# The attention output's copy one step later, and the score tails in the transposes' PSUM banks

## The chip, the cores and the metric

The kernel runs on one core of a Trainium2 chip. TensorE (PE) does the matmuls and writes them into PSUM, VectorE (DVE) finds the 32 largest scores of each row, ScalarE (ACT) copies out of PSUM and does exponentials, GpSimd (POOL) works from SBUF to SBUF, and SyncE (SP) issues nearly all DMAs. Each engine runs its own instructions strictly in the order in which they were written; engines meet only through semaphores. The metric is the device time of one execution in microseconds, as a median of several runs.

## The reference: what is computed

The first block is attention with a top-k mask, for 8 batches and 8 heads of 576 tokens of 64 channels:

```python
scores = scale * np.matmul(q, k.transpose(0, 1, 3, 2))
kth = np.partition(scores, -32, axis=-1)[..., -32:-31]
scores = np.where(scores >= kth, scores, -1e9)
attn = softmax(scores)                       # with 1e-9 added to the sum
attn_out = np.matmul(attn, v)
```

Its output, as x of 8 batches by 576 tokens by 512 channels, goes through a Fourier mix and a feed-forward block:

```python
u = x + np.real(np.fft.fft(np.fft.fft(x, axis=1), axis=2))
un = (u - mean(u)) / np.sqrt(var(u) + 1e-6)
out = u + np.maximum(un @ w_ch1, 0.0) @ w_ch2     # 512 -> 2048 -> 512
```

All of it is float32.

## The kernel before

**Tiles and steps.** Two heads of one batch form a pair: 32 pairs, 4 to a batch. A pair's query rows are cut into 9 items (IN_PAIR, line 326): four tiles of 128 rows for each of the two heads, and one item, with no head of its own (`e is None`, called the None item here), that holds the 64 leftover rows of both heads. The main loop (from line 1485) runs one step per item, 288 in all. Step i is called step r of its pair here, with r = i mod 9.

DVE needs 4 MAX8 and 3 MATCH_REPLACE8 over 576 scores for each item: it finds eight maxima at a time and strikes them out. In step i it does the second half of item i and the first half of item i+1 (line 1582). The scores are therefore made three steps ahead: step i issues `scores(i + 3)`.

**Scores.** For each item, a matmul makes the scores of the first 512 keys in one of two PSUM banks of the pool ps_s (tag "sp", line 398, or line 383 for the None item in four quarter-sized matmuls), and ACT copies them into the SBUF tile S (lines 401 and 390). The scores of the last 64 keys of both heads, the tails, come from one matmul of their own, `sp_t` (line 368), which takes a bank of the same two, and two small ACT copies (line 372). Both heads of a tile are made in one step, and their tails in the next; the None item's scores and tails are made in the same step, which is step 1 of a pair. So in step 1 the order of banks is: scores of the first half (bank A), scores of the second half (bank B), tails (bank A again). PE can write the tails only when ACT has copied both quarters of bank A.

The steps with a tails matmul are 7, 0, 1, 3 and 5 of a pair.

**Other users of PSUM.** Pool ps_t, two banks (tag "tp"), is for transposes: q and k of the next pair are transposed there by `prep` (line 294), q in step 0 and k in step 5 of a pair. Each takes four transposes into one bank and a fifth, for the leftover rows, into the other, each followed by ACT copies (line 316 for q, 318 and 322 for k). Pool ps_o, one bank (tag "o"), holds the attention's output and then its transposes. Three more banks serve the feed-forward block.

**From the mask to the attention's output.** In the first batch, in pair 7 and in the last pair, the masked and exponentiated tile P is transposed on PE through ps_t. In pairs 4 to 6 and 8 to 30 (`by_dma`, line 435) it is transposed by DMA instead. There, for an item:

- POOL scales the bounds after DVE's last maximum, at the end of step i (`bounds`, line 427, tile nt);
- in step i+1 ACT makes the mask first of all (line 443, waits for nt), POOL subtracts (line 446), and ACT takes the exponential at the end of its step (line 454);
- in step i+2, after the next item's mask, ACT splits the result into two planes of 16 bits (line 467), and SP sends them to DRAM;
- in step i+3 SP issues the transposing DMA into the tile PT (`turn`, line 501);
- at the end of step i+4, `attend` (line 559, 20 matmuls) multiplies PT with v into the bank "o". That is done for two chunks of a pair: chunk 0 (320 rows) at the end of step 8, chunk 1 (256 rows) at the end of step 3 of the next pair.

Right after `attend`, in the same step, `attended` (line 568) issues on ACT the copy of that bank into the SBUF tile xT, for chunk 0 two small copies of the denominators, and the sum with 1e-9 into rd. It also puts DVE's reciprocal of rd on a list that is run at the end of the next step. In the next step `to_tokens` (line 589) turns xT back with 3 or 2 transposes into the bank "o" (tile tpx), placed behind the scores and the transposes of q or k, and DVE multiplies them with rd into x at the end of that step (lines 603 and 610; in batch 1 ACT does it a step later). `to_tokens` is held back while x still belongs to an earlier batch that has not been written out; the chunks wait in a list (`pending`) and are taken one per step, in steps that have no `attend`.

**What ACT is given in one step**, in order: mask of the last item, the two planes of the item before it, the copies of this step's scores or tails, one-step-late work on a list `out_next` (used in the first batch alone), the copies of q or k, the copies of Fourier and feed-forward work, the exponential, and where there is an `attend` its copy last:

```python
if n == n_mask:                       # after the scores of the step
    run(i, "act")
    for fn in out_next:
        fn()
```

**The feed-forward work.** The matmuls of the Fourier mix and of the feed-forward block of a finished batch (lines 961, 988, 1027, 1158) are cut into units of about 2 us, and a planner spreads them over the steps of the next batch so that PE's work per step comes out even. It counts the costs of `attend` and `to_tokens` in the step of the `attend`. After the last item only this work is left.

Of the kernel before, what the change touches and what calls it, by code (L numbers as in the profile page):

```python
# [9 lines left out]
F32 = mybir.dt.float32  # L10
# [63 lines left out]
def kernel(  # L74
# [21 lines left out]
    NPB = H // 2  # L96
    NPAIR = B * NPB
# [23 lines left out]
    ps_s = ctx.enter_context(tc.tile_pool(name="ps_s", bufs=2, space=bass.MemoryType.PSUM))  # L121
    ps_t = ctx.enter_context(tc.tile_pool(name="ps_t", bufs=2, space=bass.MemoryType.PSUM))
# [7 lines left out]
    def bank(shape, name, hold=False):  # L130
        n = banks_free.pop(0)
        t = ps_m.tile(shape, F32, name=name, tag=f"m{n}", bufs=1)
        if not hold:
            banks_free.append(n)
            return t
        return t, lambda: banks_free.append(n)
# [19 lines left out]
    late_now, late_next = [], []  # L156
# [170 lines left out]
    PER_PAIR = len(IN_PAIR)  # L327
# [6 lines left out]
    def scores(i, part):  # L334

        if not 0 <= i < N:
            return 0.0
        pair, t, e = items[i]  # L340
        qT, kT = qT_of[pair], kT_of[pair]
        rows = ROWS[t]
        if part == 0:
            for n in range(1 if e is None else 2):
                Ssb[i + n] = attp.tile([P, S], F32, name=f"S_{i + n}", tag="S", bufs=6)
        q_cols = slice(P * t, P * t + rows)


        plain = (slice(0, NF * P), slice(NF * P, S))
        tails_first = (slice(TAIL, S), slice(0, TAIL))  # L350
        if e is None:
            to = [
                (Ssb[i], slice(TAIL * h, TAIL * (h + 1)), *(tails_first if h and by_dma(i) else plain))
                for h in range(2)
            ]
        else:
            to = [
                (Ssb[i], slice(0, P), *plain),
                (Ssb[i + 1], slice(0, P), *tails_first),
            ]  # L360
        if part == 1:

            copy = nc.scalar.copy if i else nc.vector.tensor_copy
            shape, name = [P, NF * P], f"sp_{i}_t"
            sp = ps_s.tile(shape, F32, name=name, tag="sp") if i else bank(shape, name)

            q_end = P * t + rows
            nc.tensor.matmul(  # L368
                sp[:, 0:P], lhsT=qT[:, q_end - P:q_end], rhs=kt_t, start=True, stop=True
            )  # L370
            for h, (s_t, r, _, tails) in enumerate(to):
                copy(out=s_t[r, tails], in_=sp[P - rows:P, TAIL * h:TAIL * (h + 1)])  # L372
            return 0.3
        if e is None and i >= PER_BATCH:

            half = NF * P // 2
            sps = [
                ps_s.tile([P, NF * P], F32, name=f"sp_{i}_{h}", tag="sp") for h in range(2)
            ]
            for g in range(2):  # L380
                for h in range(2):
                    hd = slice(D * h, D * (h + 1))
                    nc.tensor.matmul(
                        sps[h][TAIL * g:TAIL * (g + 1), 0:half],
                        lhsT=qT[hd, q_cols], rhs=kT[hd, half * g:half * (g + 1)],
                        start=True, stop=True,
                    )
            for h, (s_t, r, keys, _) in enumerate(to):
                for g in range(2):
                    nc.scalar.copy(  # L390
                        out=s_t[r, keys][:, half * g:half * (g + 1)],
                        in_=sps[h][TAIL * g:TAIL * (g + 1), 0:half],
                    )
            return 0.6
        for h, (s_t, r, keys, _) in enumerate(to):
            hd = slice(D * h, D * (h + 1))
            sp = ps_s.tile([P, NF * P], F32, name=f"sp_{i}_{h}", tag="sp")
            nc.tensor.matmul(  # L398
                sp[r], lhsT=qT[hd, q_cols], rhs=kT[hd, :], start=True, stop=True
            )  # L400
            nc.scalar.copy(out=s_t[r, keys], in_=sp[r])  # L401
        return 1.04
# [24 lines left out]
    def bounds(i):  # L427

        if i < N:
# [2 lines left out]
                out=Nt[i], in0=M8.pop(i)[:, 0:TOPK:TOPK - 1], in1=cc, op=ALU.mult  # L432
            )

    def by_dma(i):

        pair = i // PER_PAIR
        return NPB <= pair < NPAIR - 1 and pair != 2 * NPB - 1

    def mask(i, then=None):  # L440

        w = Wk[i]
        nc.scalar.activation(out=w, in_=Ssb[i], func=AF.Relu, scale=-FAR, bias=Nt[i][:, 1:2])  # L443
        if then is not None:
            then()
        nc.gpsimd.tensor_tensor(out=w, in0=Ssb[i], in1=w, op=ALU.subtract)  # L446
        if not by_dma(i):
            Ssb.pop(i)

    def expo(i):  # L450
        pair, t, e = items[i]
        w = Wk[i]
        c = DEN_COL[(t, e)]
        nc.scalar.activation(  # L454
            out=Ssb[i] if by_dma(i) else w, in_=w, func=AF.Exp, bias=Nt.pop(i)[:, 0:1],
            accum_out=den_t[pair % 3][:, c:c + 1],
        )
# [92 lines left out]
    def attend(pair, ch, c0=0, c1=None):  # L550

        c1 = CW[ch] if c1 is None else c1
        pt, vv = PT[pair, ch], v_of[pair]
        if c0 == 0:
            o_of[pair, ch] = ps_o.tile([P, CW[0]], F32, name=f"o_{pair}_{ch}", tag="o")
        o = o_of[pair, ch]
        for c in range(NC):
            for e in range(2):
                nc.tensor.matmul(  # L559
                    o[D * e:D * (e + 1), c0:c1],  # L560
                    lhsT=vv[:, c, e, :],
                    rhs=pt[:, NF if c == NF else (NF + 1) * e + c, c0:c1],
                    start=(c == 0),
                    stop=(c == NC - 1),
                )
        return (c1 - c0) / 115.0

    def attended(pair, ch, late):

        o, w = o_of.pop((pair, ch)), CW[ch]  # L570
        PT.pop((pair, ch))
        xT = attp.tile([P, CW[0]], F32, name=f"xT_{pair}_{ch}", tag="xT", bufs=4)
        nc.scalar.copy(out=xT[:, 0:w], in_=o[:, 0:w])
        xT_of[pair, ch] = xT
        den = den_t[pair % 3]
        if ch == 0:
            for h in range(2):
                nc.scalar.copy(
                    out=den[TH * h:TH * (h + 1), 5:6],
                    in_=den[TAIL + TH * h:TAIL + TH * (h + 1), 4:5],  # L580
                )
        c0, n = (0, 6) if ch == 0 else (6, 4)
        rd = small.tile([P, 6], F32, name=f"rd_{pair}_{ch}", tag="rd", bufs=6)

        nc.scalar.activation(out=rd[:, 0:n], in_=den[:, c0:c0 + n], func=AF.Copy, bias=1e-9)
        late.append(lambda: nc.vector.reciprocal(out=rd[:, 0:n], in_=rd[:, 0:n]))
        rd_of[pair, ch] = rd
# [699 lines left out]
    for c in range(2):  # L1287
        scores(0, c)
    prep("q", 0, ((2, NF), (NF, NC)))
    scores(2, 0)  # L1290


# [142 lines left out]
    queue, waiting, pending, written, now, out_next = [], [], [], set(), [0], []  # L1435
    step_us = 6.0

    def chunk_at(i):

        for tile in (i - 4, i - 3, i - 2):  # L1440
            r = tile % PER_PAIR
            if PER_BATCH <= tile < N and r in (4, 8):
                if i - tile == (4 if by_dma(tile) else 2 if tile == 2 * PER_BATCH - 1 else 3):
                    return tile // PER_PAIR, r // 8
        return None, None
# [38 lines left out]
    i, carry = 0, 0.0  # L1484
    while i < N + 5 or plan or queue or sums:
# [18 lines left out]
        if i < N and i % PER_PAIR == 5:  # L1504
            preps.append(lambda: prep("k", pair_of + 1))
        fixed.append(lambda: scores(j - 1, 1) if e == 1 else scores(j, 0))
        n_mask = 0
        fixed += preps
# [19 lines left out]
        if short:  # L1528
            fixed += tok
            pair, r = divmod(i - 1, PER_PAIR)  # L1530
# [39 lines left out]
        pair, ch = chunk_at(i)  # L1570
        if pair is not None:
            cost += attend(pair, ch)
            attended(pair, ch, late_next)
            pending.append((i + 1, pair, ch))
        if i < N:
            if q_step:
                load_nat("k", pair_of + 1)
# [67 lines left out]
```

## Time and profile before

| | |
|---|---|
| median of 3 runs | 1886.04 us (1885.32 to 1888.74) |
| the profiled execution | 1888.63 us |
| its span, first to last instruction | 1886.8 us |
| busy share of PE, DVE, ACT, POOL | 91%, 84%, 69%, 48% |
| DVE's work on one item, from 4 MAX8 and 3 MATCH_REPLACE8 | about 5.2 us |
| 400 to 1000 us: PE, DVE busy | 559.19 and 552.95 of 600 us |
| 1000 to 1700 us: PE, DVE busy | 681.09 and 634.93 of 700 us |
| mean granted TensorE clock | 0.954 |

The profile gives for every instruction its engine, its line in the kernel, the tile that it writes and those that it reads, its start and its duration. Where an engine stood idle before an instruction, the idle time stands in brackets behind it together with the one who ended it: "[1.64 <-ACT S L390]" means idle for 1.64 us until the ACT instruction of line 390, which writes S, was done. The view of waits sums these over a stretch: total us, number, longest. "PEld" are the weight loads of PE, which run beside its matmuls. A wait for several semaphores is put down to the one that came last. The profiled execution lies 2.6 us above the median.

### The profile page before, as it was taken

The page shows a single profiled execution, that of the slowest core. Times are in us where ns is not written, and L with a number is a line of the kernel's source. Part 1 is how long each engine was busy: PE and PEld are TensorE (multiplying, and loading weights), DVE is VectorE, ACT ScalarE, POOL GpSimd, SP SyncE. Part 2 cuts the span into 40 slices and gives each one's busy share as a digit, 9 for nine tenths or more (in the row PEclk, how much of TensorE's full clock was granted, in tenths as well). Part 3 has the DMA queues.
Part 4 walks back from the last instruction along what each step waited for, and adds up shares of the span by engine and source line. Part 5 has one row for each costly group of instructions (what it writes and reads, how often), then busy time and mean ns, then how long its engine had stood idle before and what let it go on. Part 6 is the DMA issues. An engine that isn't in the chain of part 4 may idle for free.

```text
span 1886.8 us, 26907 instructions
## 1 busy us (share of the span) xinstructions
PE 1724.3 (91%) x8134; PEld 1089.6 (58%) x8134; DVE 1582.2 (84%) x3301; ACT 1295.8 (69%) x3104; POOL 912.1 (48%) x1278
## 2 busy tenths in 40 slices
PE   6667699889899999999999999999999999999999
PEld 3344365355456654566456665566556655667677
DVE  7999999799899999997998898999999899862110
ACT  6878658577787777776777677777787678652100
POOL 4768644454745366354643465355544464341012
PEclk8778899899899999999999999999999999999999
DMA  5333026661557755575465845586467655440132
GB/s 166 103 97 108 20 63 160 166 156 32 137 149 193 186 130 137 140 202 140 122 157 136 225 121 128 142 220 156 120 160 179 179 132 144 120 117 6 51 110 72
DMA packets 516576, 249.16 MB, mean 132 GB/s; under 512 B 398288, under 2 KB 506448, under 8 KB 516432
## 3 DMA queue, kind: packets, MB, share of 16 engines
q1 hardware_dynamic: 515664, 247.23, 50.6%
q8 instruction: 65, 1.06, 0.2%
q14 instruction: 79, 0.65, 0.1%
q10 hardware_dynamic: 768, 0.21, 0.0%
HBM read 93.63 MB, written 84.74 MB: 95 GB/s over the span
## 4 chain that ended last, share of the span: by engine, by line
PE 63%; DVE 12%; ACT 10%; POOL 6%; DMA 4%; issue 3%; SPq 2%; POOLq 0%; DVEq 0%; ACTq 0%
PE hp L961 23%; PE cp L988 8%; PE o L559 7%; DVE m L422 5%; PE sp L398 5%; DVE wk L424 5%; PE cw L1158 3%; PE yp L750 3%; PE cv L1158 3%; PE cp L1027 2%; POOL wk L446 2%; ACT wk L443 2%; ACT wk L467 2%; PE sp_t L368 2%; PE mp L811 1%
## 5 line engine op out<-in xcount | busy, mean ns | idle before, releaser
L446 POOL TENSOR_TENSOR wk<-S,wk 128x576 f32<-128x576 f32 x288 | 408.6, 1419 | 572.2 <-ACT wk L443 570.0
L422 DVE MAX8 m<-wk 128x8 f32<-128x576 f32 x864 | 626.4, 749 | 6.0
L961 PE MATMUL hp<-unT,w 128*128 128x256 f32 (+1 forms) x2048 | 535.5, 412 | 3.6 <-ACT hT L965 2.8
L961 PEld LDWEIGHTS hp<-unT,w 128*128 128x128 f32 x2048 | 378.5, 191 | 134.5 <-issue 30.1
L424 DVE MATCH_REPLACE8 wk<-m,wk 128x576 f32<-128x576 f32 x576 | 427.4, 742 | 0.0
L467 ACT COPY wk<-S 128x576 uint16<-128x576 uint16 x468 | 288.7, 666 | 0.1
L443 ACT ACTIVATE wk<-S,nt 128x576 f32<-128x576 f32 x288 | 222.2, 772 | 73.0 <-POOL nt L431 72.1
L988 PE MATMUL cp<-w,hT 128*128 128x512 f32 x512 | 244.6, 614 | 0.0
L422 DVE MAX8 m<-S 128x8 f32<-128x576 f32 x288 | 213.9, 743 | 31.9 <-ACT S L372 31.8
L559 PE MATMUL o<-PT,v 128*64 128x256 f32 (+3 forms) x1440 | 205.1, 429 | 19.3 <-DMA PT<-planes 15.4
L424 DVE MATCH_REPLACE8 wk<-m,S 128x576 f32<-128x576 f32 x288 | 213.5, 741 | 0.0
L965 ACT ACTIVATE hT<-hp 128x320 f32<-128x320 f32 (+1 forms) x256 | 103.6, 409 | 155.3 <-PE hp L961 154.5
L454 ACT ACTIVATE S<-wk,nt 128x576 f32<-128x576 f32 x234 | 182.6, 781 | 39.9 <-POOL wk L446 38.9
L398 PE MATMUL sp<-kT,qT 64*128 64x512 f32 (+1 forms) x528 | 183.1, 693 | 12.2 <-ACT means L1346 5.1
L559 PEld LDWEIGHTS o<-PT,v 128*64 128x64 f32 x1440 | 118.0, 158 | 105.0 <-issue 35.5
L988 PEld LDWEIGHTS cp<-w,hT 128*128 128x128 f32 x512 | 93.4, 195 | 109.5 <-issue 107.7
L401 ACT COPY S<-sp 128x512 f32<-128x512 f32 (+1 forms) x264 | 141.6, 586 | 18.5 <-PE sp L398 17.6
L1103 POOL TENSOR_TENSOR hT<-hT 128x512 f32<-128x512 f32 x64 | 81.3, 1274 | 99.0 <-ACT hT L965 86.2
L368 PEld LDWEIGHTS sp_t<-kt,qT 128*128 128x128 f32 x320 | 55.7, 198 | 100.6 <-ACT S L390 44.2
L368 PE MATMUL sp_t<-kt,qT 128*128 128x128 f32 x320 | 72.1, 308 | 45.0 <-ACT S L390 29.8
L431 POOL TENSOR_TENSOR nt<-m,cc 128x2 f32<-128x2 f32 x288 | 58.9, 205 | 111.9 <-DVE m L422 108.9
L1158 PE MATMUL cw<-w,hT 128*128 128x256 f32 x448 | 105.7, 383 | 0.7 <-issue 0.6
(160 smaller groups left out, 2137.9 us busy)
## 6 DMA issues: line engine op xcount, KB each, us to landing
planes<-wk SPq DMA_DIRECT2D x208, 288.0 KB, 2.7
w<-w_parts SPq DMA_DIRECT2D x82, 512.0 KB, 4.7
space<-in_moe_w_ch_dram SPq DMA_DIRECT2D x32, 512.0 KB, 3.7
nat<-in_q_dram SPq DMA_DIRECT2D x128, 64.0 KB, 2.4
v<-in_v_dram SPq DMA_DIRECT2D x64, 128.0 KB, 3.0
out_dram<-x SPq DMA_DIRECT2D x32, 256.0 KB, 2.6
nat<-in_k_dram SPq DMA_DIRECT2D x62, 128.0 KB, 2.9
planes<-wk SPq DMA_DIRECT2D x52, 144.0 KB, 2.6
```

The lines of the kernel that those rows point to most:

```text
L368: nc.tensor.matmul(sp[:, 0:P], lhsT=qT[:, q_end - P:q_end], rhs=kt_t, start=True, stop=True)
L398: nc.tensor.matmul(sp[r], lhsT=qT[hd, q_cols], rhs=kT[hd, :], start=True, stop=True)
L422: ops.append(lambda src=src, m8=m8: nc.vector.max(out=m8, in_=src))
L424: ops.append(lambda src=src, m8=m8: nc.vector.match_replace(w, m8, src, NEG))
L443: nc.scalar.activation(out=w, in_=Ssb[i], func=AF.Relu, scale=-FAR, bias=Nt[i][:, 1:2])
L446: nc.gpsimd.tensor_tensor(out=w, in0=Ssb[i], in1=w, op=ALU.subtract)
L454: nc.scalar.activation(out=Ssb[i] if by_dma(i) else w, in_=w, func=AF.Exp, bias=Nt.pop(i)[:, 0:1], accum_out=den_t[pair % 3][:, c:c + 1],)
L467: nc.scalar.copy(out=words[:, half, :], in_=src[:, half, :])
L559: nc.tensor.matmul(o[D * e:D * (e + 1), c0:c1], lhsT=vv[:, c, e, :], rhs=pt[:, NF if c == NF else (NF + 1) * e + c, c0:c1], start=(c == 0) ...
L961: nc.tensor.matmul(hp[:, 0:w], lhsT=w1[:, dt, P * it:P * (it + 1)], rhs=unT[:, dt, 0:w], start=(dt == 0), stop=(dt == NDT - 1),)
L988: nc.tensor.matmul(cp, lhsT=hT[:, it, P * n:P * (n + 1)], rhs=w2[:, it, :], start=(it == 0), stop=(it == NIT - 1),)
L1158: nc.tensor.matmul(dst, lhsT=h()[a][:, kc, :], rhs=rhs_of(kc), start=start and kc == 0, stop=kc == NK - 1, skip_group_check=True,)
```

## The change

Two things change, both only in the pairs whose P is transposed by DMA.

The tails matmul takes a bank of ps_t (tag "tp"), which it then shares with the transposes of q and k, instead of one of ps_s. There are 26 such pairs with 5 tails each, 130 in all.

`attended` is no longer issued in the step of its `attend` but in the next one, after that step's scores, by way of `out_next`; `to_tokens` may come two steps after the `attend` instead of one. The last chunk of a batch keeps the old order. That moves 47 of the 52 chunks of these pairs: chunk 0's copy from the end of step 8 to step 0 and its transposes from step 0 to step 1, chunk 1's copy from the end of step 3 to step 4 and its transposes from step 4 to step 5.

```diff
-            sp = ps_s.tile(shape, F32, name=name, tag="sp") if i else bank(shape, name)
+            if by_dma(i):
+                sp = ps_t.tile(shape, F32, name=name, tag="tp")
+            else:
+                sp = ps_s.tile(shape, F32, name=name, tag="sp") if i else bank(shape, name)
...
+    def pair_by_dma(pair):
+
+        return NPB <= pair < NPAIR - 1 and pair != 2 * NPB - 1
+
     def by_dma(i):
-
-        pair = i // PER_PAIR
-        return NPB <= pair < NPAIR - 1 and pair != 2 * NPB - 1
+        return pair_by_dma(i // PER_PAIR)
...
         pair, ch = chunk_at(i)
         if pair is not None:
             cost += attend(pair, ch)
-            attended(pair, ch, late_next)
-            pending.append((i + 1, pair, ch))
+            if pair_by_dma(pair) and (pair % NPB, ch) != (NPB - 1, 1):
+                out_next.append(lambda pair=pair, ch=ch: attended(pair, ch, late_next))
+                pending.append((i + 2, pair, ch))
+            else:
+                attended(pair, ch, late_next)
+                pending.append((i + 1, pair, ch))
```

## The prediction

> **What bounds the kernel now.** I read the busy time by stretches first, then who waited for whom between 400 and 1680 us, then two timelines.
>
> Stretches (busy us and instructions of PE, PEld, DVE, ACT, POOL, then clock, DMA share, GB/s):
>
> ```profile
> 400.00:1000.00 600.00, 559.19 (x2639) 342.81 (x2638) 552.95 (x1148) 456.83 (x1103) 303.65 (x455) 0.96 0.57 143
> 1000.00:1700.00 700.00, 681.09 (x3296) 434.36 (x3295) 634.93 (x1319) 517.73 (x1236) 347.48 (x504) 0.99 0.60 152
> 1700.00:1800.00 100.00, 99.66 (x444) 67.32 (x442) 19.33 (x53) 20.71 (x52) 9.60 (x34) 1.00 0.08 27
> ```
>
> After 1700 us PE alone is busy, with a fixed remainder. So the end is PE's busy time, which the change leaves alone, plus PE's idle time: 600 - 559.19 = 40.8 us and 700 - 681.09 = 18.9 us in the two stretches where the change acts. Every us of PE idleness added or removed there shows at the end; DVE counts only where its lateness reaches PE through ACT.
>
> Waits from 400 to 1680 us (total, times, longest):
>
> ```profile
> ACT xT L573 <- PE o L559: 80.4, 34, 11.8
> ...
> ACT wk L443 <- POOL nt L431: 64.2, 47, 3.8
> DVE x L603 <- PE tpx L599: 43.2, 16, 6.6
> ...
> PE sp_t L368 <- ACT S L390: 28.1, 19, 3.6
> ...
> DVE rd L586 <- ACT rd L585: 11.2, 6, 6.7
> ...
> PE o L559 <- DMA PT<-planes: 7.5, 4, 2.7
> ```
>
> PE's largest wait is that of the tails for their bank (5.1 us more of it names L401). ACT's largest is for the attention's output: it stands at the copy that ends a step, with the next mask, planes and tails behind it. DVE's largest is for the transposes of xT. PE's wait for late PT is small itself, but sets off some of the others.
>
> **Part 1, the tails' bank.** Step 0 of pair 25, and from 1333 step 1:
>
> ```profile
> 1323.15 0.49 PE L368 MATMUL sp_t<-kt,qT 128*128 128x128 f32 x2
> ...
> 1323.48 0.71 PE L308 MATMUL tpq<-ident,nat 128*128 128x128 f32 x5
> ...
> 1326.29 0.31 ACT L372 COPY S<-sp_t 128x64 f32<-128x64 f32 x2
> ...
> 1333.40 1.52 ACT L390 COPY S<-sp 64x256 f32<-64x256 f32 x4
> ...
> 1334.21 0.49 PE L368 MATMUL sp_t<-kt,qT 128*128 128x128 f32 x2 [1.64 <-ACT S L390]
> 1334.54 1.88 PE L988 MATMUL cp<-w,hT 128*128 128x512 f32 x4
> ```
>
> Removed: I went through the 130 tails of the affected pairs in the timeline. PE's idle time before them sums to 34.3 us: 27.5 before the None items' (step 1), 6.8 before the rest. Not all of it goes. After the change the next scores, in step 2, take the two banks that the None item's copies (L390) free. At 969.02 the tails waited 2.31 us and the scores follow with no unit between, so they would inherit 1.55. Setting for each pair the start of those scores, less the wait saved, against the ends of the L390 copies, 7.9 of the 27.5 us only move and 19.6 go. Removed: 19.6 + 6.8 = 26.4 us.
>
> Added: in ps_t the tails sit next to the transposes of q (step 0) and k (step 5). Bank order there is tails, four transposes in the other bank, and the fifth in the tails' bank: a new wait on L372. At 1323 there is no unit between; the fifth transpose started at 1323.91, and L372 ended at 1326.60. Laying all 26 places of each kind side by side (end of L372 plus 0.06 us of signalling, as in the rows of L390, minus the start of the fifth transpose, where positive) gives 44.3 us for q and 11.9 for k, if ACT keeps its times. These are the upper ends; the lower is nothing, where ACT comes sooner; a gain from a later PE transpose has no row and is excluded. For q ACT does come sooner: xT's copy (0.42), two denominators (0.39) and rd (0.21) leave its way, 1.02 us, and where it idled at xT it can do mask and planes meanwhile. Subtracting 1.02 and that idleness (2.0 at most, mask plus planes) place by place leaves 17.3 us, which I take because its shift is measured. For k nothing gets shorter: ACT there waits for nt (1354.84, 3.14 us), so I take 11.9. Sum of part 1: 17.3 + 11.9 - 26.4 = +2.8 us.
>
> The Trainium skill, "Perfetto Trace Analysis", section "Matmuls", wants independent groups to rotate through different PSUM banks so that copies overlap matmuls. Here either ring has two banks, and the rows show that the new one has a tight place too; by the rule alone the change would save all 34.3 us.
>
> **Part 2, the copy and the transposes a step later.** Per chunk it moves an ACT copy (0.36 to 0.43 us), two of 0.2 (chunk 0 only), one of 0.21, a DVE reciprocal of 0.18, 3 or 2 PE transposes and 2 or 1 DVE products (on ACT in pairs 4 to 6); none is added, and no DMA. On ACT they pass the mask, two planes and the step's score copies. The planes' DMA on SP therefore issues up to 1 us sooner, more where ACT stood, as does POOL's subtraction; SP's order stays. q's copies come no later, being behind both. No wait is added on ACT: "o" is complete before the step's scores.
>
> The bank "o" is held longer. Its next user is normally the same chunk's tpx, a step later; where older chunks are queued it is an older one's tpx in the very step of the copy. At 1016.30 that has room: L372 there began at 1014.02 behind xT, so xT's copy would end near 1013.8. I cost it at nothing; without that cover it would wait about 1 us in some five places. The skill's "PSUM — Partial Sum Buffer", section "Summary: rules for kernel authors", says to evacuate promptly, which speaks against this; no row here shows a bank wait of "o" above 1 us, and by the rule I would add those 5 us.
>
> Late PT makes PE late, and then DVE waits at the transposes. Pair 16, step 0:
>
> ```profile
> 857.96 0.49 PE L368 MATMUL sp_t<-kt,qT 128*128 128x128 f32 x2
> ...
> 858.07 0.42 ACT L573 COPY xT<-o 128x320 f32<-128x320 f32 x1 [11.77 <-PE o L559]
> ...
> 859.18 0.19 DVE L586 RECIPROCAL rd<-rd 128x6 f32<-128x6 f32 x1 [6.71 <-ACT rd L585]
> ...
> 862.81 0.55 PE L599 MATMUL tpx<-ident,xT 128*128 128x128 f32 x3
> ...
> 863.40 0.42 DVE L603 TENSOR_TENSOR x<-tpx,rd 128x256 f32<-128x256 f32 x1 [4.03 <-PE tpx L599]
> ```
>
> Chunk 0's transposes move behind the scores (0.66) and about one unit (1.9 to 2.3) of step 1: 2.9 us later on PE, while DVE has 5.3 us more work before it asks. So each such stall shrinks by up to 2.4 us. Seven are of this kind (551, 601, 799, 858, 1065, 1274, 1477): 1.9 + 2.4 + 5 x 2.4 = 16.3 us. The other stalls at tpx are of chunks held back by `pending`, and stay. Chunk 1 moves behind k's transposes (0.7) and a larger share of units (0.7), 1.4 us later within its step; in five places that had less room (0.42, 1.01, 0.67, 0.66, none) this makes 4.2 us of new stalls. DVE gains 12.1 us.
>
> What reaches PE: in each later batch the next PE wait on ACT (918, 1127, 1334, 1537: some 1.65 each; 656: 1.35) comes from a mask that waits for nt, that is for DVE. With DVE up to 2.4 us earlier, these and the new waits in step 0 shrink by about 1.7 us in five batches: -8.5 us. Its ends: 0, if PE's waits are already counted in part 1, and -12.1.
>
> **Sum.** +2.8 - 8.5 = -5.7 us on the profiled execution's 1888.6 us. That stands 2.6 us above the median of 1886.0, so I put the same difference on the median: 1880.0 us.
>
> **Rivals.**
> 1. Waits only change place: the tails' waits go to the fifth transposes, and DVE's 8.5 us are the same waits counted twice. For it: 17.3 + 11.9 is close to 26.4. Against it: the 2.4 us of DVE are additional. Result +2.8 at the most, 1886 to 1889.
> 2. Slower: PE waits at the fifth transpose for L372. Place: steps 0 and 5, 52 of them. Price: up to 44.3 + 11.9 = 56.2, less 26.4, plus 4.2 of chunk 1, that is +34 us, 1920; at two thirds of that price, 37.5 + 4.2 - 26.4 = +15, 1901. It decides once those places exceed 26.4 + 8.5 = 34.9 us, 0.67 each; I took 0.56. For it: DVE-bound stretches (1323, 1356), where ACT cannot come sooner. Against: the stretches after 858, 1065, 1274, 1477, where ACT idled 5 to 12 us.
> 3. Larger gain: ACT, free during attend, has the tails copied before the fifth transpose everywhere. -26.4 - 12.1 = -38 us, 1848 as the far end, 1860 to 1870 more likely. For it: 80.4 us of ACT idleness at xT. Against: the waits for nt.
>
> **Chances and range.** Forecast 0.42, its own range 1874 to 1884 (the 8.5 us between 5 and 12.1, part 1 within 3); rival 1 0.18; rival 2 0.30; rival 3 0.10. 0.2% is 3.8 us, about what a measurement of this kernel can tell from no change. Faster: 0.37 of the forecast and rival 3, 0.47. Same: 0.05 of the forecast and rival 1, 0.23. Slower: 0.30. Both signs hold weight, so the range takes rival 3 down to 1866 and rival 2 up to 1898, leaving out a tenth on each side.
>
> **What the profile after would show.** Part 1: the wait sp_t on L390 near nothing; new waits of tpq and tpk on L372, some 17 and 12 us; scores L398 on L390 up to 8. Part 2: ACT xT on PE o near nothing, since o is done when ACT arrives; the DVE wait for rd gone; tpx stalls 43 to about 31. PE idle from 400 to 1700 about 54 instead of 59.7 us. Wrong if the fifth transposes wait over 35 us, or if stalls at tpx grow, or if PE's units settle otherwise because the planner sees the transposes' cost a step later.

## The result

The change makes the kernel slower: 1905.05 us (median of 4 runs, 1901.56 to 1911.9) against 1886.87 us (4 runs, 1885.32 to 1888.74), a ratio of 1.0098 with a 95% interval of 1.008 to 1.0115. The forecast was 1880.0 us within 1866 to 1898. The forecast named a gain, and the time lies outside its range; the second rival had named a loss, with 1901 us.

The execution profiled after took 1911.9 us, 6.9 above its median, with a span of 1910.1. The spans of the two profiled executions thus differ by 23.3 us, some 5 more than the medians do; the shifts below are read with that in mind. Line numbers grow by 3 to 5: sp_t is now L371 and its copies L375, the scores L401 and their copies L404 and L393, the mask L448, `attend` L564, tpx L604.

The stretches of the kernel after (busy us and instructions of PE, PEld, DVE, ACT, POOL, then clock, DMA share, GB/s):

```profile
400.00:1000.00 600.00, 540.19 (x2556) 336.28 (x2555) 540.17 (x1120) 441.81 (x1069) 297.14 (x448) 0.94 0.56 140
1000.00:1700.00 700.00, 674.58 (x3268) 431.62 (x3268) 637.21 (x1326) 522.17 (x1243) 346.80 (x503) 0.99 0.60 155
```

PE is idle for 59.8 us of the first and 25.4 of the second, 85.2 in all; it was 59.7 before and the forecast was about 54. DVE loses as well, mostly in the first stretch: 552.95 busy before, 540.17 now.

Waits from 400 to 1680 us in the kernel after:

```profile
ACT wk L448 <- POOL nt L434: 80.9, 59, 4.8
...
DVE m L425 <- ACT S L375: 60.8, 24, 6.7
...
DVE x L608 <- PE tpx L604: 36.2, 20, 6.3
...
ACT S L404 <- PE sp L401: 26.9, 15, 6.1
...
ACT S L375 <- PE sp_t L371: 21.9, 9, 8.7
...
PE tpk L308 <- ACT S L375: 21.6, 9, 6.7
...
PE tpq L308 <- ACT S L375: 20.3, 11, 8.3
...
PE sp L401 <- ACT S L393: 10.3, 8, 2.1
```

PE's wait of the tails for L390 has shrunk from 28.1 to 1.3 us, ACT's for "o" at xT from 80.4 to 6.3 and DVE's for rd from 11.2 to 2.2. New are PE's waits at the fifth transposes of q and k, and DVE's wait for the tails in S has more than doubled (from 270 to 1700 us 31.8 before, 72.5 now). ACT's idleness did not vanish with the copy of xT: part of it now stands at the copies of the tails and of the scores, which PE writes behind the same `attend`.

One place shows why a stop here is worse than the one removed. Step 0 of pair 9, after:

```profile
496.70 0.49 PE L371 MATMUL sp_t<-kt,qT 128*128 128x128 f32 x2
497.03 0.60 PE L308 MATMUL tpq<-ident,nat 128*128 128x128 f32 x4
...
503.77 0.78 ACT L448 ACTIVATE wk<-S,nt 128x576 f32<-128x576 f32 x1 [3.72 <-POOL nt L434]
...
505.59 0.31 ACT L375 COPY S<-sp_t 128x64 f32<-128x64 f32 x2
...
505.89 0.76 DVE L425 MAX8 m<-S 128x8 f32<-128x576 f32 x1 [1.47 <-ACT S L375]
505.95 0.48 PE L308 MATMUL tpq<-ident,nat 128*128 128x128 f32 x1 [8.32 <-ACT S L375]
```

The same step before:

```profile
498.34 0.71 PE L308 MATMUL tpq<-ident,nat 128*128 128x128 f32 x5
...
498.98 0.77 PE L750 MATMUL yp<-fs,fg 128*64 128x145 f32 x8
...
502.72 0.32 ACT L372 COPY S<-sp_t 128x64 f32<-128x64 f32 x2
...
503.02 0.76 DVE L422 MAX8 m<-S 128x8 f32<-128x576 f32 x1 [1.46 <-ACT S L372]
```

ACT can't copy the tails until its mask, which waits for nt, that is for DVE's last maximum of the step before. Before the change that copy stopped only DVE, while PE went through its Fourier units. Now PE's fifth transpose waits for the same copy, with all those units behind it. One late ACT instruction holds PE and DVE at once.

This can be counted. From the bounds of item 36 to those of item 279, in idle stretches of 0.3 us and more, PE and DVE stood idle together for 2.9 us before and 15.1 us after (worked out from the instructions of the two traces).

To see what each place costs PE in all, the trace was summed by tile over the same items (called the stage below): for each matmul the time from the end of PE's work before it to its own end, so that the wait and a slow matmul both count. "cp" is the result of the second feed-forward matmuls. In us:

| | stage | tails sp_t | tpq and tpk | scores sp | cp | all else |
|---|---|---|---|---|---|---|
| before | 1417.6 | 83.3 | 29.8 | 165.5 | 258.5 | 880.5 |
| after | 1438.2 | 39.8 | 83.7 | 156.7 | 265.8 | 892.2 |
| difference | +20.6 | -43.5 | +53.9 | -8.8 | +7.3 | +11.7 |

The tails gave back 43.5 us, of which 35.2 were waits and 8.3 the tails' own matmuls. But the fifth transposes took 53.9. These two places make +10.4 of the +20.6. At cp it is +7.3; there PE's time at a granted clock of 0.50 rose from 18.1 to 35.6 us. Of the +11.7 elsewhere, 6.7 are more idle time before `attend`. What causes these last two was not tested one by one.

### The profile page after: what moved, and what is told of

It reads as the page before. It is cut to its first block, busy times and chain, and to the rows that moved or that the text cites. A ratio compares the mean times of both kernels' runs of the same rounds, so it can differ in the third digit from the quotient of the medians.

```text
span 1910.1 us, 26930 instructions
## 1 busy us (share of the span) xinstructions
PE 1715.6 (90%) x8134; PEld 1093.0 (57%) x8134; DVE 1586.1 (83%) x3301; ACT 1295.7 (68%) x3104; POOL 912.2 (48%) x1278
## 3 DMA queue, kind: packets, MB, share of 16 engines
q8 instruction: 65, 1.06, 0.2%
## 4 chain that ended last, share of the span: by engine, by line
PE 52%; ACT 14%; DVE 11%; POOL 11%; issue 7%; DMA 3%; SPq 1%; POOLq 0%; DVEq 0%; ACTq 0%
PE hp L966 20%; PE o L564 5%; DVE wk L427 5%; PE cp L993 5%; DVE m L425 5%; POOL wk L451 4%; PE sp L401 4%; ACT wk L448 3%; ACT wk L472 3%; PE yp L755 3%; PE cw L1163 3%; PE cv L1163 3%; PE cp L1032 3%; POOL fg L651 2%; ACT S L459 2%
## 5 line engine op out<-in xcount | busy, mean ns | idle before, releaser
L448 ACT ACTIVATE wk<-S,nt 128x576 f32<-128x576 f32 x288 | 222.5, 773 | 93.9 <-POOL nt L434 91.8
L425 DVE MAX8 m<-S 128x8 f32<-128x576 f32 x288 | 214.0, 743 | 72.5 <-ACT S L375 72.5
L993 PE MATMUL cp<-w,hT 128*128 128x512 f32 x512 | 253.4, 633 | 0.0
L564 PE MATMUL o<-PT,v 128*64 128x256 f32 (+3 forms) x1440 | 201.3, 423 | 26.3 <-DMA PT<-planes 10.9
L401 PE MATMUL sp<-kT,qT 64*128 64x512 f32 (+1 forms) x528 | 169.7, 676 | 16.4 <-ACT S L393 10.3
L564 PEld LDWEIGHTS o<-PT,v 128*64 128x64 f32 x1440 | 117.9, 156 | 106.8 <-issue 40.7
L404 ACT COPY S<-sp 128x512 f32<-128x512 f32 (+1 forms) x264 | 141.4, 585 | 38.7 <-PE sp L401 38.0
L1163 PEld LDWEIGHTS cw<-w,hT 128*128 128x128 f32 x448 | 82.4, 190 | 20.9 <-issue 9.3
L527 PE MATMUL tpP<-ident,wk 128*128 128x128 f32 x216 | 41.3, 323 | 58.4 <-ACT wk L459 34.7
```

Of the source, the lines that this page charges most:

```text
L401: nc.tensor.matmul(sp[r], lhsT=qT[hd, q_cols], rhs=kT[hd, :], start=True, stop=True)
L425: ops.append(lambda src=src, m8=m8: nc.vector.max(out=m8, in_=src))
L564: nc.tensor.matmul(o[D * e:D * (e + 1), c0:c1], lhsT=vv[:, c, e, :], rhs=pt[:, NF if c == NF else (NF + 1) * e + c, c0:c1], start=(c == 0) ...
L993: nc.tensor.matmul(cp, lhsT=hT[:, it, P * n:P * (n + 1)], rhs=w2[:, it, :], start=(it == 0), stop=(it == NIT - 1),)
L1163: nc.tensor.matmul(dst, lhsT=h()[a][:, kc, :], rhs=rhs_of(kc), start=start and kc == 0, stop=kc == NK - 1, skip_group_check=True,)
```

## The experiments

Three theories stood at the start. R (ring): the tails now share two banks with the transposes right behind them, and PE waits there for the tails' copies. C (copy): the later copy of the attention's output and the later transposes cost the time. U (units): the planner spreads PE's units otherwise, because it sees costs a step later. Against U speaks already that PE's order of work before and after differs in little: 84 of its 8134 matmuls stand in another place, 57 of them the moved transposes of xT.

### Part 1 alone

```diff
-            if pair_by_dma(pair) and (pair % NPB, ch) != (NPB - 1, 1):
-                out_next.append(lambda pair=pair, ch=ch: attended(pair, ch, late_next))
-                pending.append((i + 2, pair, ch))
-            else:
-                attended(pair, ch, late_next)
-                pending.append((i + 1, pair, ch))
+            attended(pair, ch, late_next)
+            pending.append((i + 1, pair, ch))
```

> Part 1 of the change alone: the tails' matmul in the banks of the transposes, copy and transposes of the attention's output as before. Theory R (ring: the fifth transpose of q and k waits for the bank that the tails hold, and this costs the 18 us): the whole loss is here or more, since ACT is not relieved of the copy: 1900 to 1915 us against 1887, with 45 to 60 us of PE waits of tpq and tpk on the tails' copies. Theory C (copy: the later copy and transposes cost it, chunk 1's transposes standing behind those of k): no loss, 1880 to 1888 us. Theory U (units of the feed-forward block settle in other steps because the transposes' cost counts a step later): as C, 1880 to 1888 us, since here nothing of the planner's sums moves.

Measured: 1934.38 us (1927.85 to 1937.72), ratio 1.0238 (1.021 to 1.0267) to the kernel before. (All ratios here are to the kernel before run beside the experiment: 1889.43 us for this one and the next three, 1888.92 us for the last four.) Its waits from 270 to 1700 us:

```profile
ACT xT L578 <- PE o L564: 73.2, 33, 11.8
...
PE tpq L308 <- ACT S L375: 36.3, 23, 4.4
...
PE tpk L308 <- ACT S L375: 18.5, 11, 5.0
```

The whole loss is in the tails' bank; the other part softens it. The two new waits sum to 54.8 us (57.6 with the first place of q, which lies before 270 us), next to the prediction's upper ends of 44.3 + 11.9 = 56.2. That the sums agree is luck: over all its 26 places q came to 39.1, below its upper end, and k to 18.5, above what was called one. C falls as the cause of the loss, and so does U: PE's matmuls stand in the same order as before, all 8134. R's size was still underrated: the time lies above what it expected.

### Part 2 alone

```diff
-            if by_dma(i):
-                sp = ps_t.tile(shape, F32, name=name, tag="tp")
-            else:
-                sp = ps_s.tile(shape, F32, name=name, tag="sp") if i else bank(shape, name)
+            sp = ps_s.tile(shape, F32, name=name, tag="sp") if i else bank(shape, name)
```

> Part 2 alone: the copy of the attention's output in the next step and its transposes two steps on, the tails' matmul in its old banks. Theory R: no loss, a small gain of up to the 8.5 us that the prediction gave it: 1877 to 1888 us, ACT's wait for the attention's output below 15 us in place of 80 between 400 and 1680 us, PE's wait of sp_t on the None item's copies 15 to 28 us. Theory C and theory U: the loss is here, 1898 to 1910 us, with more of DVE's waits for tpx than the 43 us of before (C) or with PE idle in other places than the named waits (U).

Measured: 1886.99 us (1883.51 to 1890.58, 10 runs), ratio 0.9986 (0.9973 to 0.9999): a gain of 0.3% at the most, and by the interval almost none at the least. From 270 to 1700 us:

```profile
DVE m L422 <- ACT S L372: 44.0, 19, 6.3
DVE x L605 <- PE tpx L601: 42.1, 20, 5.3
...
ACT S L372 <- PE sp_t L368: 33.2, 13, 11.1
...
ACT S L401 <- PE sp L398: 22.3, 14, 4.8
```

ACT's wait at xT fell from 83.1 to 7.5 us, but its wait for the tails rose from 5.2 to 33.2 and that for the scores from 8.1 to 22.3. When PT is late, `attend` holds up everything that PE writes behind it, so ACT waits for the next thing instead. DVE's stalls at tpx stay (44.1 before, 42.1), and what rd no longer costs (20.6, now 3.2) comes back at the tails in S (31.8, now 44.0).

### The fifth transposes in the scores' banks

With the whole change, `prep` takes a bank of ps_s for the transpose of the leftover rows of q and k:

```diff
-            tp = ps_t.tile([P, 4, P], F32, name=f"tp{n}_{pair}_{c0}", tag="tp")
+            last_rows = c0 == NF and pair_by_dma(pair - 1)
+            tp = (ps_s if last_rows else ps_t).tile(
+                [P, 4, P], F32, name=f"tp{n}_{pair}_{c0}", tag="sp" if last_rows else "tp"
+            )
```

> The whole change, and the fifth transpose of q and of k (the leftover rows) takes a bank of the scores' pool where the tails have left it, so that the tails and the transposes of one step no longer meet in one bank. Theory R: the waits of tpq and tpk on the tails' copies go (below 5 us in place of 48), and the time falls below that of before: the 26 us of tails' waits that the prediction found removable, less what moves: 1860 to 1880 us. Theory C or U: still slow, 1895 to 1908 us, since both parts of the change are in it.

Measured: 1868.74 us (1864.95 to 1869.61), ratio 0.9891 (0.9869 to 0.9913). From 270 to 1700 us no wait of a transpose of q or k for the tails is left, and PE's first waits are:

```profile
PE o L567 <- DMA PT<-planes: 22.4, 9, 7.4
PE sp L404 <- ACT S L396: 10.3, 8, 2.1
PE sp L404 <- ACT kT L321: 7.0, 7, 2.4
```

So the whole loss goes when the fifth transposes leave the tails' ring (PE's order of matmuls is the same in both kernels), and behind it a gain of 1.1% had been hidden. The same edit with part 1 alone (the main loop as in the first experiment):

> Part 1 alone, with the fifth transpose in a bank of the scores' pool; copy as before. Theory R: 1865 to 1883 us, the tails' waits gone and no new ones; the difference to the kernel with both parts is what the later copy brings, some 0 to 9 us. Theory C: below 1887 us as well, and clearly below the kernel with both parts, by 15 us or more. Theory U: as C.

Measured: 1869.38 us (1865.69 to 1869.86), ratio 0.9892 (0.9867 to 0.9918). With the ring mended no gain or cost of the later copy can be seen. On the tight ring it was worth about 1.4% (the ratio is 1.0238 without it and 1.0098 with it). The waits of tpq are 36.3 us without it and 22.7 with it, which fits that ACT no longer stands at xT ahead of mask and tails; but tpk's rise from 18.5 to 23.2, so that the two waits explain only 8.9 of the 26 us by which the stage shortens.

### One of the two alone

The edit above with `and n == "q"`, then with `and n == "k"`, in the condition.

> The whole change, with only q's fifth transpose (step 0) in the scores' pool; k's still shares the tails' bank. Theory R, with the waits seen in the changed kernel (22.7 us before q's and 23.2 before k's fifth transpose between 270 and 1700 us): the loss halves, 1881 to 1893 us. If k's waits are the costly ones, because there ACT itself waits for POOL and DVE waits for the same copies: 1890 to 1902. If q's are: 1870 to 1880.

> The counterpart: only k's fifth transpose (step 5) in the scores' pool; q's still shares the tails' bank. Theory R with equal weight of the two: 1881 to 1893 us. If k's waits are the costly ones: 1870 to 1880. If q's are: 1890 to 1902.

Measured: q's moved, 1884.48 us (1879.69 to 1887.76), ratio 0.9969 (0.9951 to 0.9986); k's moved, 1889.41 us (1884.95 to 1892.25), ratio 0.9997 (0.998 to 1.0014). From the 1.0098 of the change, q's move takes off 1.3% and k's 1.0%, both together 2.1%: nearly a sum. The wait that is left stays what it was in the kernel after (k's 23.4 against 23.2, q's 23.2 against 22.7), so the two places do not feed each other.

### The fifth transposes last in the step

The whole change with its banks, but the fifth transpose is issued last of the step's listed work, behind the Fourier work, with feed-forward units in between:

```diff
+        split = which is not None and pair_by_dma(pair_of)
+        blocks = ((0, NF),) if split else ((0, NF), (NF, NC))
+        if which:
+            preps.append(lambda: prep(which, pair_of + 1, blocks))
...
+        if split:
+            fixed.append(lambda: 0.0 * prep(which, pair_of + 1, ((NF, NC),)))
         n_tr = len(fixed)
```

> The whole change with its banks, but in the affected pairs the fifth transpose is issued last of the step's listed work, behind the transposes of the output and the Fourier work, with feed-forward units between. Theory R in the sense that PE only lacks other work between the tails and the fifth transpose: the waits on the tails' copies fall from 46 us to below 15 and the time to 1868 to 1885 us, without any other bank. If sharing a bank is costly wherever the transpose stands: 1890 to 1905 us.

Measured: 1867.87 us (1865.74 to 1870.82), ratio 0.9883 (0.9852 to 0.9915). From 270 to 1700 us PE's wait at tpq is down to one of 1.0 us, and this is left at tpk:

```profile
PE tpk L308 <- ACT S L375: 12.5, 8, 5.0
```

Two banks are thus enough. What was missing was other work for PE between the tails and the transpose that takes their bank. (Besides the fifth transposes, 44 of the 8134 matmuls stand elsewhere than in the kernel after.) This kernel and the two with the fifth transposes in ps_s beat the kernel before by 1.1 to 1.2%; their intervals overlap, so none of them is shown to be the best.

### The fifth transposes moved in the kernel before

The same edit in `prep`, with the tails still in ps_s and the copy in its old place.

> The kernel before, with the tails in the scores' pool as they were and q's and k's fifth transposes there too, for the same pairs. It tells whether the 1.1% that the swapped kernels gained came from the tails leaving the scores' pool (then nothing is gained here and the fuller pool may cost: 1885 to 1905 us) or from the fifth transposes leaving the transposes' pool (then 1865 to 1875 us).

Measured: 1891.65 us (1886.49 to 1896.22), ratio 1.0009 (0.9993 to 1.0025). Moving the transposes by itself brings no gain; the gain of the mended kernels comes with the tails' leaving the scores' banks.

## Why the prediction was wrong

The same sum by tile as above, for three of the experiments:

| | stage | tails sp_t | tpq and tpk | scores sp | cp | all else |
|---|---|---|---|---|---|---|
| part 1 alone | 1464.2 | 41.4 | 94.5 | 159.1 | 275.6 | 893.6 |
| fifth in ps_s | 1396.3 | 39.7 | 31.5 | 166.9 | 258.6 | 899.6 |
| fifth last | 1396.6 | 39.8 | 46.2 | 157.1 | 257.3 | 896.2 |

**The failing step: "17.3 us" for q and "11.9" for k.** Over the 26 places of each, the profiled execution has 25.3 and 23.2 us of waits, 48.5 together against 29.2. (From 270 to 1700 us it is 22.7 and 23.2; in the stage 53.9 were lost, with the longer time of the transposes themselves.) The rival's threshold of 34.9 us was passed. Its mechanism was the right one, but that its 1901 us lies within about 4 us of the median is partly luck: it put these places at 37.5 us.
- For q the upper end of 44.3 was reduced by ACT's 1.02 us and by up to 2.0 us of its idleness at xT, place by place. The second reduction assumes that ACT, freed from xT, does the mask early. The mask waits for nt: ACT's wait there went from 67.3 to 83.9 us (270 to 1700 us). Where ACT waits so, the tails' copies end 2.16 to 2.17 us after nt at the earliest, in both kernels, as in pair 9 above (nt is done at 503.73, the copies at 505.90). In step 0 of pairs 9, 13, 25 and 29, which hold 16.4 of the 25.3 us, the copies came only 0 to 0.42 us sooner against nt than before, and in pair 9 PE came 4.2 us earlier.
- For k the figure went by the times of the kernel before, and that moved too. It was called an upper end "if ACT keeps its times". ACT kept them, counted from nt; PE came earlier to the same copy. Step 5 of pair 25 before, then after:

```profile
1354.84 0.78 ACT L443 ACTIVATE wk<-S,nt 128x576 f32<-128x576 f32 x1 [3.14 <-POOL nt L431]
1355.26 0.71 PE L308 MATMUL tpk<-ident,nat 128*128 128x128 f32 x5
...
1356.66 0.31 ACT L372 COPY S<-sp_t 128x64 f32<-128x64 f32 x2
```

```profile
1372.37 0.60 PE L308 MATMUL tpk<-ident,nat 128*128 128x128 f32 x4
...
1373.26 0.77 ACT L448 ACTIVATE wk<-S,nt 128x576 f32<-128x576 f32 x1 [3.14 <-POOL nt L434]
...
1375.07 0.31 ACT L375 COPY S<-sp_t 128x64 f32<-128x64 f32 x2
...
1375.44 0.48 PE L308 MATMUL tpk<-ident,nat 128*128 128x128 f32 x1 [2.46 <-ACT S L375]
```

Before, PE's transposes began 0.42 us behind the mask; after, 0.89 us ahead of it. Step 5 of pairs 13, 17, 21, 25 and 29 holds 17.4 of k's 23.2 us, where the laying gave 6.7. There the fourth transpose ended 1.04 to 1.06 us after nt before, and 0.23 to 4.44 us ahead of nt after. With part 2 alone it ended 1.05 to 1.78 us after nt, and with part 1 alone in four of the five places earlier than before. So it is part 1, the tails' other bank, that lets PE come early (worked out from the instructions of the four traces).

**The tails' "26.4 us removed" came true in waits.** The 34.3 us before the 130 tails all went; the 3.2 us that the profile still has at sp_t from 270 to 1700 us (38.4 before) belong to pair 7, which the change leaves alone. The 7.9 us said to move to the next scores showed as predicted: 2.2 before, 10.3 after, at L401 for L393. That leaves 26.2. The 8.3 us of the tails' own matmuls were not in the sum: behind a stop the first matmul of a tail adds 0.38 us to PE's time, without one 0.17, where it overlaps the matmul ahead of it (32 and 103 cases in the stage before).

**The premise "PE's busy time, which the change leaves alone" was wrong.** The same 8134 matmuls are recorded as 1724.3 us busy before, 1715.6 after and 1703.4 with the fifth transposes in ps_s. In the stage, in us:

| | stage | PE idle | PE busy | of that at a granted clock of 0.50 |
|---|---|---|---|---|
| before | 1417.6 | 80.6 | 1337.0 | 85.2 |
| after | 1438.2 | 107.0 | 1331.2 | 89.7 |
| part 1 alone | 1464.2 | 116.4 | 1347.9 | 105.8 |
| fifth in ps_s | 1396.3 | 78.1 | 1318.2 | 71.8 |
| fifth last | 1396.6 | 82.3 | 1314.3 | 64.5 |

The loss after is idle time, +26.4 us. But the gain of the mended kernels is hardly idle time: the tails' waits are gone, yet almost as much idleness has come up elsewhere (before `attend` 17.9 us before and 29.8 with the fifth in ps_s, before the scores 9.1 and 20.5). What has shrunk is the busy time, by 18.8 and 22.7 us, in good part that at half clock. A stop of PE costs more than its idle time. In the kernel before, around one wait of the tails (PE's timeline, then two stretches with columns as above):

```profile
969.02 0.80 PE L368 MATMUL sp_t<-kt,qT 128*128 128x128 f32 x2 [2.31 <-ACT S L390]
969.78 3.39 PE L398 MATMUL sp<-kT,qT 64*128 64x512 f32 x4
```

```profile
966.00:970.00 4.00, 1.69 (x9) 1.14 (x8) 3.97 (x10) 3.93 (x10) 1.55 (x2) 0.83 0.18 53
970.00:974.00 4.00, 4.00 (x5) 1.28 (x6) 3.86 (x12) 3.92 (x10) 1.90 (x10) 0.50 0.51 123
```

The granted clock fell to 0.50 within the stop of 2.31 us (a mean of 0.83 puts the fall 1.4 us before 970), and four score matmuls took 3.39 us, 1.06 to 1.22 each. In the stage of the kernel before, 402 of the 432 score matmuls with 512 columns are recorded at 0.5 to 0.7 us; 27 have 0.9 us or more there, 10 after and 6 with the fifth transposes in ps_s.

The Trainium skill, "TensorE: Matmul & The Clock Gate", section "Part 1: The HAM clock gate", says that an idle window of about 3.4 us halves the PE clock and that a busy window restores it. The row above agrees with the halving, though the stop itself was only 2.31 us of a stretch in which PE was busy for 1.69 of 4.

**DVE's "-8.5 us" did not come.** The seven stalls at tpx were to shrink by 16.3 us; the sum fell from 44.1 to 36.2 (270 to 1700 us), and rd's 20.6 to 2.2. But the wait for the tails in S rose by 40.7. Part 2 alone shows the step's own fault: DVE's time there moved to the tails in S, its idle stretches in the stage summed to 96.8 us against 95.0 before, and the time was 0.9986 of before. The 2.4 us per batch were freed only until the next scores, which are late because the same `attend` is late.

**The bank "o", "costed at nothing", was right.** With the ring mended, the kernels with and without the later copy differ by 0.6 us, within both ranges. The skill's rule in "PSUM — Partial Sum Buffer", section "Summary: rules for kernel authors", to evacuate promptly would have added the 5 us named in the prediction; these runs do not show them: from 270 us on, no transpose of xT waits 0.4 us or more for the copy in the kernel after, one does in part 2 alone (0.8 us) and one with the fifth last (2.2 us).

**"The planner settles otherwise", left open, is not the cause.** Part 1 alone keeps PE's order of matmuls and loses most, and the mended kernel with the planner's costs a step later and the one without are equal.

**The third rival's size**, 1860 to 1870 us, is what the mended kernels reach, but not by its way: there the fifth transposes do not wait because they take another bank or come later, not because ACT comes sooner. (The forecast's 1886.0 less 5.7 is 1880.3, not 1880.0; nothing hangs on it.)

## What to carry to other kernels

Before a tile is given another ring of banks, look at who allocates from that ring next in program order and what PE can do between the two: moving a tile whose copy is late to a ring where the next allocation follows at once cost 48.5 us of waits here, and putting either the next allocation in another ring or the intervening work ahead of it turned +1.0% into -1.1%. When such a wait is laid out from a trace, ask of both sides whether the change moves them: the side that waits can come earlier, as PE did for k (23.2 us where 11.9 was called the upper end), and the side that releases can come sooner only if it waits for nothing else; ACT's idleness in one place is no slack if its next instruction waits for DVE. And a time taken away from one engine's wait is gained only if the next thing that it needs is ready by then.

## What the runs showed of the hardware

Two things had not been expected. First, short stops of PE were followed by a lower clock. In the kernel before, between 270 and 1690 us, the granted clock fell to 0.50 during each of the 11 stops of 2 us and more or within 3 us of its end, though eight of them were shorter than 3.4 us; of the 16 stops between 1 and 2 us, 4 had such a fall. In the kernel after it was 14 of 17 stops of 2 us and more (worked out from the traces). Second, the recorded busy time of the same 8134 matmuls in the same order varies by 20.7 us between kernels that differ only in banks (1727.1 for part 1 alone, 1706.4 for it with the fifth transposes in ps_s), so that busy plus idle can't be summed as if the first were fixed. Lower clock and lost overlap behind stops are what the traces show of its causes; how the rest divides is not shown.
